# One-token attention over K and V of 537 MB: q spread by one matmul, half of K's sums in one PSUM bank, a third halving on VectorE, shared buffers

## Chip, cores and metric

One core of one Trainium2 chip runs the kernel; the other cores are idle. The metric is the device time of one execution in microseconds. The trace is one profiled execution; its span (1250.2 us before) is some 1.6 us shorter than the time of the same run.

## The reference

```python
B, H, Sq, Skv, Dh = 8, 32, 1, 4096, 128          # bf16
scores = einsum('bhqd,bhkd->bhqk', q, k) * Dh ** -0.5
out = einsum('bhqk,bhkd->bhqd', softmax(scores), v)
```

There are 256 independent heads with one query each. K and V are 268 MB each, and every byte is used once.

## The kernel before

A tile is 8 heads: 16 partitions per head, 256 positions in each partition, so K of a tile is [128, 256, 128] and 8.39 MB. There are 32 tiles and three slots for K and V together. VectorE multiplies K by q in place, halves the sum over d by additions, TensorE adds the rest with an identity matrix into PSUM (its output memory, used here in banks of 512 f32 values per partition), VectorE reduces each PSUM bank to scores, and ScalarE makes the weights. A loop on TensorE multiplies V by them. In the listing, `...` marks cuts.

```python
def q_prep(t):                       # q of 8 heads: pick, copy, spread, copy
    x, p0 = divmod(t * G, P)
    qh = ps_q.tile([G, D], F32, name="qh", tag="qp")
    nc.tensor.matmul(qh[:], lhsT=ident[:, p0 : p0 + G], rhs=q_all[:, x, :], start=True, stop=True)
    qg = q_pool.tile([G, D], BF16, name="qg", tag="qg")
    nc.scalar.activation(out=qg[:], in_=qh[:], func=ACT.Copy)
    qp = ps_q.tile([P, D], F32, name="qp", tag="qp")
    nc.tensor.matmul(qp[:], lhsT=heads..., rhs=qg[:], start=True, stop=True)
    ...
def width_of(t, u):                  # columns left for TensorE
    return D // 4 if u >= NU // 2 and 0 < t < NT - 3 else D // 2
def product(t, lo, hi):              # VectorE, in place in K
    ... part *= q
    ... part[:, :, 0:64] += part[:, :, 64:128]
    if width_of(t, lo // UC) < D // 2:
        ... part[:, :, 0:32] += part[:, :, 32:64]
def sum_over_d(t, u):                # 64 positions x 8 columns = one bank
    for s in range(width_of(t, u) // DS): nc.tensor.matmul(ps[:], lhsT=ident[:], rhs=...)
def scores_of(t, u):                 # 64 scores from one bank
    nc.vector.tensor_reduce(out=scs[t][:, u * UC : (u + 1) * UC], in_=..., axis=AX.X, op=ALU.add)
...
for t in range(NT):                  # tiles 1 to 29 ("loop")
    product(t, 0, 2 * Q); result_of(t - 2); q_prep(t + 2)
    sum_over_d(t, 0); sum_over_d(t, 1)
    product(t, 2 * Q, 3 * Q); sum_over_d(t, 2); scores_of(t, 0); scores_of(t, 1)
    product(t, 3 * Q, C); sum_over_d(t, 3); scores_of(t, 2)
    values_loop(t - 1); load("k", t + 1); load("v", t)
    scores_of(t, 3); weights_of(t); copy_of(t - 1)
```

## Time and profile before

| | before |
|---|---|
| time, median of 6 runs | 1251.88 us (1251.49 to 1252.03) |
| busiest engine | VectorE, 1021.9 us, 82% |
| loads | 536.94 MB, 99.5% of 16 engines' time |
| waiting of VectorE for K | 139.9 us in 28 tiles |

In the views, PE is TensorE, DVE VectorE, ACT ScalarE, POOL GpSimd, SPq the queue of SyncE from which the loads are issued, and L191 line 191 of the kernel; a name after `<-` in brackets is what ended the idle time. The prediction below shows the page's main lines. Views are added. First, the groups of instructions with shapes kept apart; the columns are instructions, busy us and mean ns, idle us before them. The prediction takes its 2292 ns from this line:

```profile
L194 DVE TENSOR_TENSOR kt<-kt 128x4096 bf16<-128x4096 bf16 x70 | 160.5, 2292 | 2.4
```

Second, two small queues of the page (packets, MB, share of 16 engines), called instruction, which move no data of the kernel.

```profile
q8 instruction: 15, 0.25, 0.1%
...
q14 instruction: 9, 0.07, 0.0%
```

Third, the timeline at the end of tile 15 (start, duration, idle before with its releaser). VectorE finishes its last addition at 616.46, reduces the third quarter, and then waits 1.35 us for the four matmuls of the fourth:

```profile
615.24 1.22 DVE L199 TENSOR_TENSOR kt<-kt 128x2048 bf16<-128x2048 bf16 x1
616.38 0.68 DVE L223 TENSOR_REDUCE sc<-ps 128x64 f32<-128x512 f32 x1
...
618.41 0.69 DVE L223 TENSOR_REDUCE sc<-ps 128x64 f32<-128x512 f32 x1 [1.35 <-PE ps L211]
```

### The profile page before, as it was taken

How to read it: one execution, taken by the hardware profiler on the slowest of the kernel's cores; microseconds unless marked ns; L12 is line 12 of the kernel's file. 1: busy time of each engine (PE TensorE's matmuls, PEld its weight loads, DVE VectorE, ACT ScalarE, POOL GpSimd, SP SyncE). 2: the span in 40 equal slices, each digit the busy share in tenths (PEclk: the TensorE clock that was granted, in tenths of full speed). 3: DMA queues.
4: the chain of work that ended last, by engine and by line, in shares of the span. 5: the costliest groups of instructions: out<-in, count | busy, mean ns of one | idle time of the engine just before them, and what ended most of it. 6: DMA issues, size and time to landing. Idle time of an engine off the chain costs nothing. (4 is left out here: it accounts for less than half of the span.)

```text
span 1250.2 us, 10842 instructions
## 1 busy us (share of the span) xinstructions
PE 786.8 (63%) x3116; PEld 299.6 (24%) x3116; DVE 1021.9 (82%) x495; ACT 166.1 (13%) x433; POOL 4.5 (0%) x24
## 2 busy tenths in 40 slices
PE   3366567666576655766558665577655776556755
PEld 1122123222232222322223222222222222212222
DVE  7887987878977789777798777987779877798783
ACT  0111011111011110111101111011110111101111
POOL 1000000000000000000000000000000000000000
PEclk9987788777888778877788777887778878779867
DMA  9999999999999999999999999999999999999997
GB/s 405 436 436 435 434 436 432 436 430 428 426 437 436 429 435 434 434 435 436 436 434 432 424 437 437 432 430 428 436 437 434 430 433 434 430 435 421 427 446 329
DMA packets 11432, 537.33 MB, mean 430 GB/s; under 512 B 1808, under 2 KB 2064, under 8 KB 2320
## 3 DMA queue, kind: packets, MB, share of 16 engines
q1 hardware_dynamic: 11072, 536.94, 99.5%
q8 instruction: 15, 0.25, 0.1%
q10 hardware_dynamic: 336, 0.07, 0.0%
q14 instruction: 9, 0.07, 0.0%
HBM read 536.94 MB, written 0.07 MB: 430 GB/s over the span
## 5 line engine op out<-in xcount | busy, mean ns | idle before, releaser
L191 DVE TENSOR_TENSOR kt<-kt,qb 128x8192 bf16<-128x8192 bf16 (+1 forms) x99 | 560.9, 5665 | 146.6 <-DMA kt<-in_k_dram 139.9
L211 PE MATMUL ps<-kt,ident 128*128 128x512 bf16 x800 | 278.4, 511 | 389.9 <-DVE kt L199 299.7
L294 PE MATMUL av<-vt,w 128*32 x1740 | 425.5, 397 | 4.6
L194 DVE TENSOR_TENSOR kt<-kt 128x4096 bf16<-128x4096 bf16 (+1 forms) x99 | 288.8, 2917 | 3.4
L294 PEld LDWEIGHTS av<-vt,w 128*32 x1740 | 173.4, 100 | 262.4 <-issue 119.5
L211 PEld LDWEIGHTS <-ident 128*128 128x128 bf16 x800 | 95.7, 120 | 565.4 <-issue 527.9
L223 DVE TENSOR_REDUCE sc<-ps 128x64 f32<-128x512 f32 x128 | 85.3, 685 | 54.0 <-PE ps L211 54.0
L248 ACT ACTIVATE e<-sc,nmax 128x256 bf16<-128x256 f32 x32 | 16.3, 508 | 706.7 <-DVE nmax L242 706.7
L255 ACT ACTIVATE w<-e,mine 128x256 bf16<-128x256 bf16 x256 | 105.6, 495 | 1.1
L199 DVE TENSOR_TENSOR kt<-kt 128x2048 bf16<-128x2048 bf16 x56 | 68.6, 1225 | 1.9
L351 ACT ACTIVATE comb<-av 32x512 bf16<-32x512 f32 (+1 forms) x32 | 18.8, 586 | 329.0 <-PEq L284 321.4
L280 PE MATMUL av<-vt,w 128*32 128x512 bf16 x116 | 47.2, 499 | 14.6 <-issue 13.1
L371 PE MATMUL op<-comb,pick 32*16 32x128 bf16 (+1 forms) x128 | 12.1, 213 | 20.7 <-ACT comb L351 20.7
L280 PEld LDWEIGHTS av<-vt,w 128*32 128x32 bf16 x116 | 6.9, 100 | 55.2 <-issue 55.2
L177 PE MATMUL qp<-qg,heads 8*128 8x128 bf16 x32 | 7.0, 217 | 16.7 <-ACT qg L175 16.7
L371 PEld LDWEIGHTS <-pick 32*16 32x16 bf16 (+1 forms) x128 | 8.7, 83 | 27.7 <-issue 27.3
L322 PE MATMUL av<-vt,w 128*32 128x512 bf16 x188 | 13.7, 418 | 2.3 <-DMA vt<-in_v_dram 2.3
L235 DVE TENSOR_REDUCE pmax<-sc 128x1 f32<-128x256 f32 x32 | 13.4, 420 | 1.1
L175 ACT ACTIVATE qg<-qh 8x128 bf16<-8x128 f32 x32 | 8.5, 266 | 33.5 <-PE qh L171 33.5
L171 PE MATMUL qh<-q_all,ident 128*8 128x128 bf16 x32 | 7.2, 225 | 8.7 <-DMA q_all<-in_q_dram 8.3
L179 ACT ACTIVATE qb<-qp 128x128 bf16<-128x128 f32 x32 | 8.9, 278 | 9.7 <-PE qp L177 9.7
L237 DVE TENSOR_SCALAR spread<-same,pmax 128x32 f32<-128x32 f32 x32 | 7.7, 242 | 1.1
(31 smaller groups left out, 47.7 us busy)
## 6 DMA issues: line engine op xcount, KB each, us to landing
kt<-in_k_dram SPq DMA_DIRECT2D x4, 4096.0 KB, 24.3
kt<-in_k_dram SPq DMA_DIRECT2D x4, 2048.0 KB, 13.0
vt<-in_v_dram SPq DMA_DIRECT2D x1, 4096.0 KB, 33.9
vt<-in_v_dram SPq DMA_DIRECT2D x1, 2048.0 KB, 38.5
vt<-in_v_dram SPq DMA_DIRECT2D x1, 1024.0 KB, 40.5
vt<-in_v_dram SPq DMA_DIRECT2D x1, 512.0 KB, 41.3
vt<-in_v_dram SPq DMA_DIRECT2D x31, 25.8
kt<-in_k_dram SPq DMA_DIRECT2D x29, 28.3
```

Of the source, the lines that this page charges most:

```text
L191: nc.vector.tensor_tensor(out=part, in0=part, in1=qb[:].to_broadcast([P, hi - lo, D]), op=ALU.mult)
L194: nc.vector.tensor_tensor(out=part[:, :, 0 : D // 2], in0=part[:, :, 0 : D // 2], in1=part[:, :, D // 2 : D], op=ALU.add,)
L199: nc.vector.tensor_tensor(out=part[:, :, 0 : D // 4], in0=part[:, :, 0 : D // 4], in1=part[:, :, D // 4 : D // 2], op=ALU.add,)
L211: nc.tensor.matmul(ps[:], lhsT=ident[:], rhs=kt[:, u * UC : (u + 1) * UC, s * DS : (s + 1) * DS], start=(s == 0), stop=(s == n - 1),)
L223: made = nc.vector.tensor_reduce(out=scs[t][:, u * UC : (u + 1) * UC], in_=sums.pop((t, u))[:], axis=AX.X, op=ALU.add)
L248: nc.scalar.activation(out=e[:], in_=sc[:], func=ACT.Exp, bias=nmax[:, 0:1], scale=scale, accum_out=esums[t // R][:, t % R : t % R + 1],)
L255: nc.scalar.activation(out=w[:, :, g, :], in_=e_g, func=ACT.Copy, scale=mine[:, 0, g : g + 1])
L280: pe.matmul(av, lhsT=wf[:, i * nw : (i + 1) * nw], rhs=vf[:, i * nv : (i + 1) * nv], **how)
L294: pe.matmul(av, lhsT=wf[:, bass.ds(ow + i * nw, nw)], rhs=vf[:, bass.ds(ov + i * nv, nv)], start=False, stop=False,)
L322: nc.tensor.matmul(avs[t][j * AG : (j + 1) * AG, :], lhsT=w[:, i, :, :], rhs=vt[:, c0 : c0 + CB, :], start=(i < TG), stop=(j not in group[ ...
L351: nc.scalar.activation(out=comb[0:n, :, :], in_=av[0:n, :, :], func=ACT.Copy)
L371: nc.tensor.matmul(ops[n][:], lhsT=pick[0:e, m, r, :], rhs=comb[0:e, m, :], start=(r == 0 and m == 0), stop=(r == R - 1 and m == CB - 1 an ...
```

## The change

Its intent: less TensorE and ScalarE work for q, fewer VectorE reductions, shorter TensorE sums at the end of a tile. The new q layout takes more space per partition, which the shared buffers pay for.

```diff
-    q_n = ... "(x p) d -> p x d", p=P
+    q_n = ... "(x p) d -> p x d", p=QP            # QP = 32
-    heads = consts.tile([G, G, PH], BF16, name="heads")
+    heads = consts.tile([QP, QP, PH], BF16, name="heads")
 def q_prep(t):
-    (matmul from ident, copy to qg, matmul from heads)
+    nc.tensor.matmul(qp[:], lhsT=heads[:, h0 : h0 + G, :]..., rhs=q_all[:, x, :], start=True, stop=True)
-    return D // 4 if u >= NU // 2 and 0 < t < NT - 3 else D // 2
+    return D // 8 if lo >= C // 2 and 0 < t < NT - 3 else D // 2
 def product(t, lo, hi):
+    n = D
+    while n > width_of(t, lo):
+        n //= 2
+        (add the upper n columns to the lower n)
 def sum_over_d(t, lo, hi):
+    ds = BANK // (hi - lo)                         # 128 positions x 4 columns in one bank
     ...
-    e: tag "e", comb: tag "comb", w_last: a constant, q_pool of 3
+    e and comb: tag "ec", w_last: tag "sc" of the scores, q_pool of 2
 for t in range(NT):                                # loop tiles
-    sum_over_d(t, 0); sum_over_d(t, 1) ... scores_of(t, 0); scores_of(t, 1)
+    sum_over_d(t, 0, HALF)             ... scores_of(t, 0, HALF)
-    q_prep(t + 2)
+    q_prep(t + 1)
```

More of the change, by code (lines that the diff above doesn't have):

```diff
@@ L43 @@
     scale = float(D) ** -0.5
-    UC = 64
-    DS = 512 // UC
-    NU = C // UC
+    BANK = 512
     CB = 4
@@ L49 @@
     NQ = NT // R
+    QP = 32
     TB = 32
@@ L53 @@
     assert (NV - 2 * EDGE) % LOOP == 0
-    assert LAST % CB == 0 and TG * AG == P and NH % P == 0 and P % G == 0 and TB % PH == 0 and C % CB == 0
-    q_n = q.rearrange("b h o d -> (b h o) d").rearrange("(x p) d -> p x d", p=P)
+    assert LAST % CB == 0 and TG * AG == P and NH % QP == 0 and QP % G == 0 and TB % PH == 0 and C % CB == 0
+    q_n = q.rearrange("b h o d -> (b h o) d").rearrange("(x p) d -> p x d", p=QP)
     o_n = out.rearrange("b h o d -> (b h o) d").rearrange("(n u x) d -> n x u d", u=OB, x=RG)
@@ L62 @@
     consts = ctx.enter_context(tc.tile_pool(name="consts", bufs=1))
-    q_pool = ctx.enter_context(tc.tile_pool(name="q_pool", bufs=3))
+    q_pool = ctx.enter_context(tc.tile_pool(name="q_pool", bufs=2))
     w_pool = ctx.enter_context(tc.tile_pool(name="w_pool", bufs=2))
@@ L72 @@
     ps_z = ctx.enter_context(tc.tile_pool(name="ps_z", bufs=1, space=bass.MemoryType.PSUM))
-    q_all = consts.tile([P, NH // P, D], BF16, name="q_all")
+    q_all = consts.tile([QP, NH // QP, D], BF16, name="q_all")
     ident = consts.tile([P, P], BF16, name="ident")
@@ L81 @@
     )
-    heads = consts.tile([G, G, PH], BF16, name="heads")
+    heads = consts.tile([QP, QP, PH], BF16, name="heads")
     nc.gpsimd.memset(heads[:], 0.0)
     nc.gpsimd.affine_select(
-        out=heads[:], in_=heads[:], pattern=[[-1, G], [0, PH]], compare_op=ALU.not_equal,
+        out=heads[:], in_=heads[:], pattern=[[-1, QP], [0, PH]], compare_op=ALU.not_equal,
         fill=1.0, base=0, channel_multiplier=1,
@@ L128 @@
     )
-    w_last = consts.tile([P, LAST, RG], BF16, name="w_last")
-    nc.gpsimd.memset(w_last[:], 0.0)
     loads = {}
@@ L168, in q_prep @@
     def q_prep(t):
-        x, p0 = divmod(t * G, P)
-        qh = ps_q.tile([G, D], F32, name="qh", tag="qp")
+        x, h0 = divmod(t * G, QP)
+        qp = ps_q.tile([P, D], F32, name="qp", tag="qp")
         nc.tensor.matmul(
-            qh[:], lhsT=ident[:, p0 : p0 + G], rhs=q_all[:, x, :], start=True, stop=True
-        )
-        qg = q_pool.tile([G, D], BF16, name="qg", tag="qg")
-        nc.scalar.activation(out=qg[:], in_=qh[:], func=ACT.Copy)
-        qp = ps_q.tile([P, D], F32, name="qp", tag="qp")
-        nc.tensor.matmul(qp[:], lhsT=heads[:].rearrange("g h x -> g (h x)"), rhs=qg[:], start=True, stop=True)
+            qp[:], lhsT=heads[:, h0 : h0 + G, :].rearrange("h g x -> h (g x)"), rhs=q_all[:, x, :],
+            start=True, stop=True,
+        )
         qb = q_pool.tile([P, 1, D], BF16, name="qb", tag="qb")
@@ L180, in q_prep, with width_of @@
         qbs[t] = qb
-    def width_of(t, u):
-        return D // 4 if u >= NU // 2 and 0 < t < NT - 3 else D // 2
+    def width_of(t, lo):
+        return D // 8 if lo >= C // 2 and 0 < t < NT - 3 else D // 2
     def product(t, lo, hi):
@@ L193, in product, with sum_over_d, scores_of @@
         )
-        nc.vector.tensor_tensor(
-            out=part[:, :, 0 : D // 2], in0=part[:, :, 0 : D // 2],
-            in1=part[:, :, D // 2 : D], op=ALU.add,
-        )
-        if width_of(t, lo // UC) < D // 2:
+        n = D
+        while n > width_of(t, lo):
+            n //= 2
             nc.vector.tensor_tensor(
-                out=part[:, :, 0 : D // 4], in0=part[:, :, 0 : D // 4],
-                in1=part[:, :, D // 4 : D // 2], op=ALU.add,
+                out=part[:, :, 0:n], in0=part[:, :, 0:n], in1=part[:, :, n : 2 * n], op=ALU.add
             )
     sums = {}
-    def sum_over_d(t, u):
+    def sum_over_d(t, lo, hi):
         kt = loads["k", t]
-        ps = ps_s.tile([P, UC, DS], F32, name="ps", tag="ps")
-        n = width_of(t, u) // DS
+        ps = ps_s.tile([P, BANK], F32, name="ps", tag="ps")
+        ds = BANK // (hi - lo)
+        n = width_of(t, lo) // ds
         for s in range(n):
             nc.tensor.matmul(
-                ps[:], lhsT=ident[:],
-                rhs=kt[:, u * UC : (u + 1) * UC, s * DS : (s + 1) * DS],
+                ps[:], lhsT=ident[:], rhs=kt[:, lo:hi, s * ds : (s + 1) * ds],
                 start=(s == 0), stop=(s == n - 1),
             )
-        sums[t, u] = ps
+        sums[t, lo] = ps
     scs = {}
-    def scores_of(t, u):
-        if u == 0:
+    def scores_of(t, lo, hi):
+        if lo == 0:
             scs[t] = sc_pool.tile([P, C], F32, name="sc", tag="sc")
+        ps = sums.pop((t, lo))[:].rearrange("p (c s) -> p c s", c=hi - lo)
         made = nc.vector.tensor_reduce(
-            out=scs[t][:, u * UC : (u + 1) * UC], in_=sums.pop((t, u))[:], axis=AX.X, op=ALU.add
+            out=scs[t][:, lo:hi], in_=ps, axis=AX.X, op=ALU.add
         )
-        if u == NU - 1:
+        if hi == C:
             behind_loop(made)
@@ L246, in weights_of @@
             esums[t // R] = small.tile([P, R], F32, name="esum", tag="esum")
-        e = o_pool.tile([P, C], BF16, name="e", tag="e")
+        e = o_pool.tile([P, C], BF16, name="e", tag="ec")
         nc.scalar.activation(
@@ L259, in weights_of @@
         if t == NT - 1:
+            w_last = sc_pool.tile([P, LAST, RG], BF16, name="w_last", tag="sc")
+            nc.gpsimd.memset(w_last[:], 0.0)
+            ws["last"] = w_last
             for i in range(LAST // CB):
@@ L347, in copy_of @@
     def copy_of(t):
-        comb = o_pool.tile([P, CB, D], BF16, name="comb", tag="comb")
+        comb = o_pool.tile([P, CB, D], BF16, name="comb", tag="ec")
         av = avs.pop(t)[:].rearrange("p (m d) -> p m d", d=D)
@@ L363, in last_rows @@
                 nc.tensor.matmul(
-                    ops[n][:], lhsT=w_last[:, i, :], rhs=loads["v", t][:, C - LAST + i, :],
+                    ops[n][:], lhsT=ws["last"][:, i, :], rhs=loads["v", t][:, C - LAST + i, :],
                     start=False, stop=(i == LAST - 1),
@@ L392, in store_of @@
             nc.scalar.dma_start(o_n[s, :, lo : u + 1, :], stages[s][:, lo : u + 1, :])
-    Q = C // 4
+    Q, HALF = C // 4, C // 2
     load("k", 0)
@@ L399 @@
         q_prep(0)
-        q_prep(1)
         for t in range(NT):
@@ L408 @@
                 load("v", t)
-            product(t, 0, 2 * Q if loop else Q)
-            if not loop:
-                sum_over_d(t, 0)
+            if loop:
+                product(t, 0, HALF)
+            else:
+                product(t, 0, Q)
+                sum_over_d(t, 0, Q)
             if 0 < t - 1 <= LT:
@@ L416 @@
                     result_of(t - 2)
-            if t + 2 < NT:
-                q_prep(t + 2)
+            if t + 1 < NT:
+                q_prep(t + 1)
             if loop:
-                sum_over_d(t, 0)
+                sum_over_d(t, 0, HALF)
             else:
-                product(t, Q, 2 * Q)
-            sum_over_d(t, 1)
-            if not loop:
-                scores_of(t, 0)
-            product(t, 2 * Q, 3 * Q)
-            sum_over_d(t, 2)
+                product(t, Q, HALF)
+                sum_over_d(t, Q, HALF)
+                scores_of(t, 0, Q)
+            product(t, HALF, HALF + Q)
+            sum_over_d(t, HALF, HALF + Q)
             if loop:
-                scores_of(t, 0)
-            scores_of(t, 1)
+                scores_of(t, 0, HALF)
+            else:
+                scores_of(t, Q, HALF)
             if t > 2 and t % R == 1:
                 recip_of(n)
-            product(t, 3 * Q, C)
-            sum_over_d(t, 3)
-            scores_of(t, 2)
+            product(t, HALF + Q, C)
+            sum_over_d(t, HALF + Q, C)
+            scores_of(t, HALF, HALF + Q)
             if loop:
@@ L441 @@
                 values_of(t - 1, 0, C)
-            scores_of(t, 3)
+            scores_of(t, HALF + Q, C)
             weights_of(t)
```

## The prediction

> **What bounds the kernel now.** I read the page from the top: busy shares, slices, DMA queues, then the groups of instructions, and after that the waits, the waits of the DMA queue, and the timeline of one tile.
>
> ```profile
> span 1250.2 us, 10842 instructions
> PE 786.8 (63%) x3116; PEld 299.6 (24%) x3116; DVE 1021.9 (82%) x495; ACT 166.1 (13%) x433; POOL 4.5 (0%) x24
> ...
> DMA  9999999999999999999999999999999999999997
> GB/s 405 436 436 435 434 436 432 436 430 428 426 437 436 429 435 434 434 435 436 436 434 432 424 437 437 432 430 428 436 437 434 430 433 434 430 435 421 427 446 329
> ...
> q1 hardware_dynamic: 11072, 536.94, 99.5%
> ```
>
> No compute engine is full: VectorE, the busiest, works 82% of the span. The row DMA has a 9 in every slice but the last, the loads' queue fills 99.5% of the time of 16 engines, and the rate is 421 to 437 GB/s from slice to slice. The loads are K and V, 2 x 256 x 4096 x 128 x 2 bytes = 536.9 MB, each byte read once. So the kernel looks bound by the volume of its loads.
>
> The packet records of the trace say it more sharply. Most of the volume comes in packets of 65536 bytes, whose median time is 2.42 us (5th to 95th percentile 2.418 to 2.427). Each of 16 engines moves 33.55 MB, which is 512 such packets: 512 x 2.42 = 1239 us. Counting packets in flight from record to record, all 16 engines have one from about 2 us after the start to about 1242 us. The rest of the 1250 us is the head (1 to 2 us until the first packets move), the tail (the engines run dry between 1242 and 1246 us, then the last rows of V, one copy and one store, some 5 us) and a few packets of up to 3.8 us. I put the dips of the GB/s row down to those packets and to where a slice cuts a long packet.
>
> VectorE does wait, and for what is telling:
>
> ```profile
> DVE kt L191 <- DMA kt<-in_k_dram: 139.9, 28, 6.3
> ...
> DVE sc L223 <- PE ps L211: 54.0, 33, 3.9
> ```
>
> In 28 tiles VectorE waits on average 5.0 us for the next K to land. It is ahead of the loads.
>
> What would make the change matter all the same is a load queue that runs empty because a buffer comes free late. There are three slots for K and V, so a load is issued when a slot is released. The timeline of a middle tile shows the two releases:
>
> ```profile
> 616.51 1.86 PE L211 MATMUL ps<-kt,ident 128*128 128x512 bf16 x4 [8.15 <-DVE kt L199]
> ...
> 618.41 0.33 SPq L158 DMA_DIRECT2D vt<-in_v_dram  x1
> ...
> 624.96 8.69 DVE L191 TENSOR_TENSOR kt<-kt,qb 128x16384 bf16<-128x16384 bf16 x1 [4.88 <-DMA kt<-in_k_dram]
> ...
> 635.26 0.33 SPq L158 DMA_DIRECT2D kt<-in_k_dram  x1
> ```
>
> V is issued at 618.41, the moment that the last TensorE sums have read K of this tile. The K ahead of it in the queue lands only at 624.96. Likewise K at 635.26 follows the loop over V. Setting the bytes issued against the bytes moved by then (issue times against packet records): 2.3 MB, or 5.3 us of work, are left when V is issued, and 3.4 MB, or 7.8 us, when K is. Over all steady tiles the smaller margin goes from 5.4 down to 3.6 us. It is never zero. Hence the queue does not run dry, and VectorE could be up to about 3 us per tile later before anything is lost.
>
> **What the Trainium skill says.** "DMA: Bandwidth & Descriptors", section "Where 436 GB/s comes from", derives a ceiling of 435.2 GB/s for the 16 ports into SBUF. The trace agrees: 2.42 us per 65536 bytes is 27.1 GB/s per engine, 433 GB/s for 16. "HBM Reference", section "Specifications (TRN2)", says that a core streaming alone goes well above its share of 358 GB/s, to about 425; here the mean is 430. "VectorE: DVE Perf Modes", section "Side-by-side: where the cycles go for N=2048 bf16", gives 1224 ns for 2048 elements at two per cycle; the trace has 1225 ns for the 128x2048 addition. For the new load of q, "DMA: Bandwidth & Descriptors", section "Why a DMA increments its semaphore by 16 and not by 1", says that the number of engines is the largest divisor up to 16 of the slowest dimensions: 32 partitions still give 16 engines; no run yet shows it.
>
> **The change part by part.** Durations are from these groups of the page:
>
> ```profile
> L191 DVE TENSOR_TENSOR kt<-kt,qb 128x8192 bf16<-128x8192 bf16 (+1 forms) x99 | 560.9, 5665 | 146.6 <-DMA kt<-in_k_dram 139.9
> L211 PE MATMUL ps<-kt,ident 128*128 128x512 bf16 x800 | 278.4, 511 | 389.9 <-DVE kt L199 299.7
> ...
> L223 DVE TENSOR_REDUCE sc<-ps 128x64 f32<-128x512 f32 x128 | 85.3, 685 | 54.0 <-PE ps L211 54.0
> ...
> L199 DVE TENSOR_TENSOR kt<-kt 128x2048 bf16<-128x2048 bf16 x56 | 68.6, 1225 | 1.9
> ...
> L175 ACT ACTIVATE qg<-qh 8x128 bf16<-8x128 f32 x32 | 8.5, 266 | 33.5 <-PE qh L171 33.5
> L171 PE MATMUL qh<-q_all,ident 128*8 128x128 bf16 x32 | 7.2, 225 | 8.7 <-DMA q_all<-in_q_dram 8.3
> ```
>
> 1. *Third halving on VectorE.* In tiles 1 to 28, both quarters of the second half get an addition of 64x16 = 1024 elements: 56 instructions. The 4096-element one takes 2292 ns and the 2048-element one 1225 ns; the difference is 0.521 ns per element, so 1024 elements should take 1225 - 1024 x 0.521 = 691 ns. That is +38.7 us of VectorE.
> 2. *First half in one bank.* In the 29 loop tiles two reductions of 512 inputs become one of 512 inputs to 128 outputs. I keep 685 ns, since the inputs are as many: 29 x 685 = -19.9 us of VectorE. The TensorE work stays: 16 matmuls of 512 columns either way.
> 3. *Fewer sums on TensorE.* 56 quarters go from 4 matmuls to 2: L211 falls from 800 to 688. The groups of four last 1.02 to 1.86 us in the timeline, about 0.36 us each: some -40 us of TensorE.
> 4. *q.* 32 matmuls (-7.2 us) and 32 copies on ScalarE (-8.5 us) go. At the start, the first multiplication waits for q's chain (until 9.53 us) and would begin about 0.6 us sooner; behind it the queue still holds both K tiles and a V, so no load comes sooner by it in a way that counts.
> 5. *Shared buffers.* The exponentials and the copy of the output sums share one buffer, q has two instead of three, and the zeroed weights for the last rows are made in the buffer of the last scores. The copy follows the eight weight scalings on the same engine, ScalarE, and the next exponential comes some 20 us after TensorE has read the copy; q is still prepared one tile ahead; the zeroing (302 ns) falls between the exponential (ending about 1234.2) and the last weights (about 1237.6). I expect no wait from any of them. Space is freed, but the slots for K and V stay three.
>
> Sum: VectorE 1021.9 + 38.7 - 19.9 = about 1041 us, TensorE about 740, ScalarE about 158. For the moment at which V is issued within a tile: + 2 x 0.69 (two halvings) - 0.685 (one reduction) - 0.85 (two matmuls less between the last addition and the release, at the 0.43 us spacing of the slow clock there) = -0.16 us, nearly nothing. The margin of about 5 us stays, no packet goes sooner or later, and the time stays: 1251.7 us.
>
> **The rivals.** *VectorE becomes the bound.* For it: it was the fullest engine and gets 19 us more. Against it: 0.65 us per tile against 5.0 us of waiting for K, and part of the wait for TensorE (54.0 us in total) shrinks too. If my estimate of the small addition were short by a factor of three, the margin would just be used up, and the time would rise by perhaps 5 to 30 us. *The kernel gets faster because TensorE or VectorE releases slots earlier.* For it: SP waits for them all the time. Against it: SP waits with work still queued, so an earlier issue only lengthens the queue; even a perfect stream needs 1239 us plus head and tail, so over 2% (below 1226.8 us) is shut off. *The sharing makes a new wait*, say the next exponential behind the copy of the sums: it would have to cost over 3 us per tile to show. *q on 32 partitions is slower to load:* 64 KB in 256 rows as before; doubling its packets' time would cost well under 1 us once.
>
> **Range and chances.** The runs of before spread by 0.4 us. Slow packets can differ by a microsecond or two from run to run, and the head and the tail could move by 1 us. That gives 1249.5 to 1254.0. Faster by over 2% would need fewer bytes or faster packets: 0.01. Slower by over 2% needs over 25 us from a wait I did not see: 0.02. The same: 0.97.
>
> **What would show it.** Right: DMA at 9 in all slices but the last, q1 near 99.5%, the wait of L183 (the multiplication's new line) for K still 130 to 155 us, the small additions at about 690 ns x56, 99 reductions, VectorE near 1041 us and the sums 688. Wrong: a reduction of 128x128 well over 685 ns, an addition near 1.2 us, a wait for K that vanishes while the DMA row shows gaps, or any long wait of ScalarE for the reader of the shared buffer.

## The result and the profile after

The changed kernel takes 1253.14 us (1252.68 to 1253.37, 6 runs) against 1251.88 us. The ratio is 1.001 with a 95% interval of 0.9997 to 1.0023: the same.

The page after, in the order of the first lines of the prediction (span, busy time of the engines, then by slice the DMA share in tenths and the rate, then the queues):

```profile
span 1251.0 us, 10646 instructions
...
PE 745.7 (60%) x2972; PEld 278.6 (22%) x2972; DVE 1043.5 (83%) x522; ACT 157.6 (13%) x401; POOL 5.3 (0%) x24
...
DMA  9999999999999999999999999999999999999997
GB/s 404 436 436 434 434 436 432 436 436 428 423 432 434 437 434 432 430 436 436 434 434 436 433 430 432 434 436 434 430 426 434 436 435 430 434 428 428 430 445 318
...
q1 hardware_dynamic: 11072, 536.94, 99.4%
...
q14 instruction: 10, 0.08, 0.0%
```

The row DMA has not moved by a digit. VectorE has 21.6 us more, TensorE 41.1 us less, ScalarE 8.5 us less, and the time does not follow any of them.

The groups after, shapes kept apart:

```profile
L201 PE MATMUL ps<-kt,ident 128*128 128x512 bf16 x688 | 240.4, 506 | 448.4 <-DVE kt L189 448.1
...
L189 DVE TENSOR_TENSOR kt<-kt 128x1024 bf16<-128x1024 bf16 x56 | 38.7, 692 | 1.9
L213 DVE TENSOR_REDUCE sc<-ps 128x128 f32<-128x512 f32 x29 | 19.8, 683 | 0.0
...
L166 PE MATMUL qp<-q_all,heads 32*128 32x128 bf16 x32 | 7.3, 229 | 8.6 <-DMA q_all<-in_q_dram 8.6
```

The new addition takes 692 ns, 56 times; the new reduction makes twice the scores in 683 ns.

The waits after (total us, times, longest):

```profile
DVE kt L183 <- DMA kt<-in_k_dram: 139.3, 28, 6.1
...
DVE sc L213 <- PE ps L201: 30.8, 33, 4.0
```

VectorE waits as long for K as before (139.9); its wait for TensorE has fallen from 54.0 to 30.8 us. The timeline of the same tile shows both sides of that exchange:

```profile
617.38 0.68 DVE L213 TENSOR_REDUCE sc<-ps 128x64 f32<-128x512 f32 x1
617.51 1.03 PE L201 MATMUL ps<-kt,ident 128*128 128x512 bf16 x2 [8.27 <-DVE kt L189]
618.58 0.33 SPq L153 DMA_DIRECT2D vt<-in_v_dram  x1
618.59 0.69 DVE L213 TENSOR_REDUCE sc<-ps 128x64 f32<-128x512 f32 x1 [0.53 <-PE ps L201]
...
624.99 8.69 DVE L183 TENSOR_TENSOR kt<-kt,qb 128x16384 bf16<-128x16384 bf16 x1 [4.73 <-DMA kt<-in_k_dram]
```

VectorE reaches the end of the tile 1.00 us later (617.38 against 616.38), TensorE then needs 1.03 us in place of 1.86, and V is issued at 618.58 against 618.41. The next K lands when it did.

### The profile page after: what moved, and what is told of

Its sections match the earlier page's. It is cut to its first block, busy times and chain, and to the rows that moved or that the text cites. A ratio compares the mean times of both kernels' runs of the same rounds, so it can differ in the third digit from the quotient of the medians.

```text
span 1251.0 us, 10646 instructions
## 1 busy us (share of the span) xinstructions
PE 745.7 (60%) x2972; PEld 278.6 (22%) x2972; DVE 1043.5 (83%) x522; ACT 157.6 (13%) x401; POOL 5.3 (0%) x24
## 5 line engine op out<-in xcount | busy, mean ns | idle before, releaser
L201 PE MATMUL ps<-kt,ident 128*128 128x512 bf16 x688 | 240.4, 506 | 448.4 <-DVE kt L189 448.1
L288 PE MATMUL av<-vt,w 128*32 x1740 | 429.8, 406 | 2.3
L189 DVE TENSOR_TENSOR kt<-kt 128x4096 bf16<-128x4096 bf16 (+3 forms) x211 | 396.2, 1878 | 7.2
L288 PEld LDWEIGHTS av<-vt,w 128*32 x1740 | 177.7, 102 | 260.1 <-issue 106.6
L201 PEld LDWEIGHTS <-ident 128*128 128x128 bf16 x688 | 72.1, 117 | 597.5 <-DVE kt L189 476.7
L213 DVE TENSOR_REDUCE sc<-ps 128x64 f32<-128x512 f32 (+1 forms) x99 | 67.9, 686 | 30.8 <-PE ps L201 30.8
L166 PE MATMUL qp<-q_all,heads 32*128 32x128 bf16 x32 | 7.3, 229 | 8.6 <-DMA q_all<-in_q_dram 8.6
L316 PEld LDWEIGHTS <-w 128*32 128x32 bf16 x188 | 6.2, 104 | 10.8 <-issue 7.8
L232 DVE TRANSPOSE_TENSOR_REDUCE nmax<-spread 128x1 f32<-128x32 f32 x32 | 6.8, 212 | 1.1
(27 smaller groups left out, 30.8 us busy)
```

Source lines behind the costliest of these rows:

```text
L189: nc.vector.tensor_tensor(out=part[:, :, 0:n], in0=part[:, :, 0:n], in1=part[:, :, n : 2 * n], op=ALU.add)
L201: nc.tensor.matmul(ps[:], lhsT=ident[:], rhs=kt[:, lo:hi, s * ds : (s + 1) * ds], start=(s == 0), stop=(s == n - 1),)
L213: made = nc.vector.tensor_reduce(out=scs[t][:, lo:hi], in_=ps, axis=AX.X, op=ALU.add)
L288: pe.matmul(av, lhsT=wf[:, bass.ds(ow + i * nw, nw)], rhs=vf[:, bass.ds(ov + i * nv, nv)], start=False, stop=False,)
L316: nc.tensor.matmul(avs[t][j * AG : (j + 1) * AG, :], lhsT=w[:, i, :, :], rhs=vt[:, c0 : c0 + CB, :], start=(i < TG), stop=(j not in group[ ...
```

## The experiments

Theory: the loads bind, and neither the VectorE work added nor the TensorE work removed lies on the path. Rival A: VectorE, the fullest engine, is as good as the bound. Rival B: the change saves real compute time that only this kernel's loads hide. Rival C: the 1.2 us between the medians, outside both spreads although inside the interval, come from a part of the change. Twelve kernels ran; medians of before beside them were 1251.55 to 1251.88 us.

### More VectorE work ahead of the release of K

In tiles 1 to 28, N extra instructions in the third quarter, on 64 positions x 64 columns of K. They take the maximum of each value with itself, so the result stays right, although the first halving still reads these columns (the expectation's "result unused" is not exact):

```diff
 def product(t, lo, hi):
     ...
+    if 0 < t < NT - 3 and lo == C // 2:
+        for _ in range(N):
+            nc.vector.tensor_tensor(out=part[:, :, D // 2 : D], in0=part[:, :, D // 2 : D],
+                in1=part[:, :, D // 2 : D], op=ALU.max)
```

N = 1: 

> The changed kernel with one extra VectorE instruction of 4096 elements (about 2.29 us, result unused) in tiles 1 to 28, ahead of the release of K: 28 x 2.29 = 64 us more VectorE work. Theory (the loads bound, VectorE has some 5 us per tile to spare, the smallest margin of the load queue is 3.4 us): time unchanged, 1252 to 1254.5 us, wait for K falls from 5.0 to about 2.7 us per tile. Rival (VectorE at 83% is as good as the bound): 1253 + 64 = 1317 us.

N = 2: 

> Two extra instructions, 4.6 us per tile. Theory: the wait for K falls to about 0.4 us per tile and the smallest queue margins (3.4 us) are overrun, so this is at the edge: 1253 to 1275 us. Rival (VectorE bound): 1253 + 128 = 1381 us. Rival (VectorE can never matter because the loads run by themselves): 1253 us.

N = 3: 

> Three extra instructions, 6.9 us per tile, more than the 5.0 us of waiting. Theory: VectorE is now the bound and adds (6.9 - 5.0) x 28 = 53 us: 1290 to 1325 us, no wait for K left. Rival (VectorE bound from the start): 1253 + 192 = 1445 us. Rival (never matters): 1253 us.

N = 4: 

> Four extra instructions, 9.2 us per tile. Theory: (9.2 - 5.0) x 28 = 117 us more, 1350 to 1390 us, that is 64 us over three of them: from the kink on every microsecond counts in full. Rival (VectorE bound from the start): 1253 + 256 = 1509 us. Rival (never matters): 1253 us.

| N | VectorE added per tile | time, median of 4 (N = 0: of 6) | over the changed kernel | ratio to before, 95% |
|---|---|---|---|---|
| 0 | 0 | 1253.14 us | 0 | 0.9997 to 1.0023 |
| 1 | 2.3 us | 1262.75 us | 9.6 us | 1.0067 to 1.0101 |
| 2 | 4.6 us | 1284.95 us | 31.8 us | 1.0240 to 1.0301 |
| 3 | 6.9 us | 1312.59 us | 59.5 us | 1.0476 to 1.0511 |
| 4 | 9.2 us | 1374.28 us | 121.1 us | 1.0962 to 1.0998 |

The full addition of rival A (64 us per step) is seen only from N = 3 to N = 4, where it is 61.7 us. Up to there most of the work is absorbed. N = 3 and N = 4 came out in the ranges of the theory. N = 1 and N = 2 did not: 8 and 10 us above the upper ends. The waits of N = 1, then of N = 3:

```profile
DVE kt L183 <- DMA kt<-in_k_dram: 73.6, 25, 4.5
```

```profile
DVE kt L183 <- DMA kt<-in_k_dram: 1.9, 5, 0.9
```

At N = 1 VectorE still waits 73.6 us for K, so it is not the bound, and yet the kernel is slower. The loads themselves have become slower. The packet records say how. I count packets of 65536 bytes that took over 2.7 us (the median is 2.42), their excess over 2.42 us divided by 16 engines, and the time for which engines have no packet, as a mean over the 16 (18.3 us in the changed kernel, nearly all of it before the program's first load and after the last):

| kernel | long packets | of them within 4 us after a V is issued | excess per engine | engines without a packet |
|---|---|---|---|---|
| before | 28 | 9 | 1.0 us | 17.0 us |
| changed | 24 | 5 | 0.8 us | 18.3 us |
| N = 1 | 225 | 181 | 9.4 us | 20.3 us |
| N = 2 | 397 | 330 | 16.1 us | 35.3 us |
| N = 3 | 428 | 412 | 18.4 us | 60.1 us |

The last column is counted from the first packet of the trace to its last. The two columns account for the growth of the traces' spans: at N = 1 they grow by 8.6 and 2.0 us, 10.6 against 10.9; at N = 2 by 15.3 and 17.0, 32.3 against 34.2; at N = 3 by 17.6 and 41.8, 59.4 against 58.9. At N = 1 the queue never ran empty as a whole: at the V of tiles 3 to 28 the backlog (bytes issued and not yet moved, packets in flight counted in part) was still 1.3 to 3.2 us, against 3.3 to 4.9 in the changed kernel. At N = 2 it went down to 0.1, and at N = 3 it was never above 0.2. My margin was wrong as a measure. A backlog that is an average over 16 engines is used up for some of them sooner.

The traces bear this out. At N = 3, after the V issued at 613.23, the first 16 packets start 0.95 to 1.57 us later and take 2.57 to 3.41 us, and the next 16 take 2.42 or 2.43: what is long is the first packet of each engine that had run dry. The trace shows 16 completions for each load, one by one. Of the 448 of K (16 in each of 28 tiles), 6 come less than 2.5 us after the issue of V in the kernel before (or ahead of it), 6 in the changed one, 169 at N = 1, 403 at N = 2 and all 448 at N = 3, beside 9, 5, 181, 330 and 412 long packets near a V. The limit of 2.5 us was chosen afterwards, and the packet records don't name their engine, so the two counts can't be matched engine by engine.

### The same work after the release of K

To separate late issue from VectorE's own traffic in memory, about as much work was put where VectorE waits anyway, on the scores after their last reader:

```diff
             weights_of(t)
+            if 0 < t < NT - 3:
+                for _ in range(5):
+                    nc.vector.tensor_tensor(out=sc[:], in0=sc[:], in1=sc[:], op=ALU.max)
```

> One extra instruction ahead of the release of K cost 9.7 us where none was expected, and most of the lengthened packets came within 4 us of the issue of a V. This run gives VectorE about as much extra work (5 instructions of 256 f32 elements, some 0.42 us each, 2.1 us per tile in 28 tiles), but after the release of K, in the time in which it waits for the next K anyway. Theory (a V issued later reaches the engines that are ahead too late; VectorE's work as such costs nothing): 1252.4 to 1254.5 us, some 40 lengthened packets as in the changed kernel, the wait for K down to about 2 us per tile. Rival (VectorE's traffic in memory slows the packets): about 1260 us and hundreds of lengthened packets.

It took 1252.91 us (1252.72 to 1253.03, 5 runs), ratio 1.0009. Its busy time and its wait for K:

```profile
PE 748.8 (60%) x2972; PEld 279.3 (22%) x2972; DVE 1103.1 (88%) x662; ACT 157.6 (13%) x401; POOL 5.3 (0%) x24
```

```profile
DVE kt L183 <- DMA kt<-in_k_dram: 56.3, 28, 3.3
```

VectorE has 59.6 us more than in the changed kernel, works 88% of the span as at N = 1 (1107.6 us), and waits 2.0 us per tile for K. The time has not moved, and 32 packets are long (12 near a V; 8 completions of K come less than 2.5 us after its issue). The "some 40 in the changed kernel" of the expectation is 24 by the count above. So the 10 us of N = 1 come from when V is issued. They do not come from how much VectorE does. Its traffic is not held equal here: these instructions are in f32, elsewhere, and move fewer bytes (15 KB per partition and tile against 24 KB, two inputs and the output counted). But at N = 1 the extra instruction starts 17.0 us before V is issued, and only 5 of the 225 long packets overlap it in time.

### Without the loads

The middle loads are left out and the first tiles' buffers used again. The result is wrong (relative error 1.07). A plainer cut, half of each load, reads what was never written.

```diff
     def load(kind, t):
+        if 1 < t < NT - 2 and kind == "k":
+            loads[kind, t] = loads[kind, t - 2]; return
+        if 0 < t < NT - 2 and kind == "v":
+            loads[kind, t] = loads[kind, 0]; return
```

In the kernel before: 

> The kernel before, but K of tiles 2 to 29 and V of tiles 1 to 29 are not loaded: the buffers of the first tiles are used again (wrong result on purpose). Theory (loads bound, compute needs about 33.7 us per tile against 38.7 of the loads): about 1085 us, 1060 to 1120. Rival (VectorE or TensorE bound): hardly below 1240 us.

In the changed kernel: 

> The same cut made in the changed kernel. Theory: the change is nearly neutral for the compute chain as well, -0.16 us per tile: 2 to 10 us below the kernel before with the same cut. Rival (the change saved real time that the loads hide): over 20 us below. Rival (the added VectorE work of 19 us counts in full): 15 to 25 us above.

In the changed kernel with `D // 4` for `D // 8`, so two halvings: 

> The same cut in the changed kernel with two halvings in place of three in the second half (the first half keeps its one bank). Theory: VectorE loses 38.7 us of additions and gets some 23 us of waiting for the longer TensorE sums back: about 16 us below the changed kernel with the cut, so the third halving costs more than it saves where loads don't bind. Rival (the third halving pays by relieving TensorE): above the changed kernel with the cut.

| | time, median of 4 |
|---|---|
| before, without the loads | 1114.30 us (1112.77 to 1114.68) |
| changed, without the loads | 1107.14 us (1106.30 to 1107.96) |
| changed, two halvings, without the loads | 1089.84 us (1088.98 to 1091.03) |

All are in the ranges set, though the first lies near the upper end of its own. The loads cost 138 us of the 1252: compute alone, with the last tiles' loads, needs 1114. Busy time and the wait of VectorE for the sums, in the order of the table:

```profile
PE 753.2 (68%) x3116; PEld 290.1 (26%) x3116; DVE 1019.5 (92%) x495; ACT 166.3 (15%) x433; POOL 4.5 (0%) x24
...
DVE sc L229 <- PE ps L217: 60.5, 44, 3.9
```

```profile
PE 699.0 (63%) x2972; PEld 268.3 (24%) x2972; DVE 1040.1 (94%) x522; ACT 157.8 (14%) x401; POOL 5.3 (0%) x24
...
DVE sc L219 <- PE ps L207: 31.4, 34, 4.0
```

```profile
PE 731.5 (67%) x3084; PEld 277.8 (26%) x3084; DVE 1001.4 (92%) x466; ACT 157.8 (15%) x401; POOL 5.3 (0%) x24
...
DVE sc L219 <- PE ps L207: 55.2, 34, 4.1
```

From the first to the second, VectorE works 20.6 us more and waits 29.1 us less: -8.5 us, and -7.2 was measured. From the second to the third it works 38.7 us less and waits 23.8 us more: -14.9 us, and -17.3 was measured. So the loads do hide a gain, but of 7 us. The third halving costs more than it saves. The rest of the change gains 24.5 us (1114.30 to 1089.84): the reductions' busy time falls by 18.3 us (86.3 to 68.0) and the wait for the sums by 5.3, which points to the one bank for the first half; the new q and the sharing were not tried alone without the loads.

### Parts of the change, with the loads

All with 5 rounds. The control is the changed kernel unaltered. One kernel has only the new q and the shared buffers (`D // 4`, two banks for the first half), one has only the sums (q and buffers as before), one undoes the third halving:

```diff
-        return D // 8 if lo >= C // 2 and 0 < t < NT - 3 else D // 2
+        return D // 4 if lo >= C // 2 and 0 < t < NT - 3 else D // 2
```

Control: 

> The changed kernel again, as a control for the difference of 1.2 us. Theory (a real difference of 0.1%, of the order of one slow engine in the tail): 1252.7 to 1253.4 us again, against 1251.5 to 1252.0 for before. Rival (chance of one session): within 0.4 us of before.

New q and sharing only: 

> Only the new q (one matmul from 32 partitions) and the shared buffers; sums and halvings as in the kernel before. If the 1.2 us come from q's load or from sharing: 1253 us. If they come from the sums: 1251.9 us. In both cases within 2 us of before, since the loads bind.

Sums only: 

> Only the sums: first half in one bank, three halvings in the second half; q and the buffers as in the kernel before. If the 1.2 us come from the sums: 1253 us. If they come from q or sharing: 1251.9 us. VectorE again near 1043 us busy, and no effect of it on the time.

Two halvings: 

> The changed kernel with two halvings in place of three: VectorE does 38.7 us less work, TensorE 112 matmuls more. Theory (loads bind): 1252 to 1253.5 us, the wait for K grows by some 0.6 us per tile to about 156 us in total. Rival (VectorE bound): about 1215 us.

| kernel | time, median of 5 | ratio to before, 95% |
|---|---|---|
| changed, again | 1252.84 us (1252.42 to 1253.00) | 0.9993 to 1.0020 |
| new q and sharing only | 1252.76 us (1252.60 to 1253.04) | 0.9994 to 1.0021 |
| sums only | 1252.49 us (1252.38 to 1252.63) | 0.9992 to 1.0019 |
| two halvings | 1251.59 us (1251.41 to 1251.75) | 0.9984 to 1.0011 |

By the intervals all four are the same as before (1251.82 us, 9 runs). The control fell in the theory's range. The two halvings came out 0.4 us below theirs. Taking 38.7 us off VectorE left the time where it was. The wait for K took up 17.1 us of it, the wait for the longer TensorE sums the rest (30.8 to 54.4 us):

```profile
DVE kt L183 <- DMA kt<-in_k_dram: 156.4, 29, 6.9
```

That ends rival A. As to rival C, neither half of the change carries the 1 us alone: each half has it, and the kernel with both but with two halvings has not. My either-or expectation failed. What does go with it is a count. The small queue q14 moves 8192 bytes now and then, and two series of such packets appear in every trace. Of one series, each packet (0.32 us) stands next to a load packet of 3.08 us in place of 2.42 (2.97 once, at 146 us of the kernel before). For the last ones, at 1152 and 1205 us, the neighbour is a packet of 32768 bytes, of 1.87 to 1.88 us in place of 1.21. That delays one DMA engine by some 0.98 us each time:

| trace | this series, us from the start | last packet of V lands |
|---|---|---|
| before | 146, 418, 707, 998 | 1246.20 us |
| two halvings | 146, 418, 707, 1000 | 1246.23 us |
| changed | 127, 379, 651, 901, 1152 | 1247.14 us |
| changed, again | 126, 379, 651, 901, 1152 | 1247.03 us |
| sums only | 127, 379, 651, 901, 1152 | 1247.05 us |
| new q and sharing only | 146, 418, 668, 940, 1205 | 1247.19 us |
| work after the release | 105, 321, 552, 785, 979 | 1246.98 us |

Four such packets go with 1246.2 us, five with 1247.0 to 1247.2. The completions of one load by the 16 engines lie 0.3 us apart in the first transfers. In the changed kernel the last falls behind the first by 3.3 us before the packet at 901 and by 4.2 after it, by 3.6 before that at 1152 and by 4.6 after it; in the kernel before, which has none at 1152, the distance stays at 3.6. The last engine sets the end. The Trainium skill ("DMA: Bandwidth & Descriptors", section "Queues, rings and completion order") calls queue row 14 runtime-internal. The page of the trace calls it instruction. That the fifth packet is the cause fits all seven traces but was not tried by itself (the other small queue, q8, has 14 packets with the two halvings as in the slower ones), and which engine's program asks for these packets stays open.

No version beats the kernel before. The one with two halvings equals it here.

## Why the prediction was right

**What bounds.** Right. The volume of the loads fixes the time: the row DMA stays at 9, and 38.7 us less VectorE work gives nothing.

**The parts.** The addition was put at 691 ns and took 692; the reduction at 685 and took 683. The sums went to 688 matmuls and lost 38.0 us against 40 predicted; TensorE as a whole came to 745.7 us and not 740, with 4.3 us more in the loop over V (425.5 to 429.8). ScalarE came out at 157.6 us. VectorE was put at 1041 us and came to 1043.5: 85.3 us of reductions became 67.9, a saving of 17.4 and not of 19.9, since the records of neighbouring reductions overlap and two in a row were already counted short. q's chain began the first multiplication at 9.20 us against 9.53, 0.3 us sooner and not 0.6, because q landed 0.3 us later. No wait for the shared buffers appeared.

**The moment at which V is issued.** The sum said -0.16 us; in the tile shown V comes 0.17 us later by the clock, and 0.14 us later relative to the landing of K. The two matmuls saved 0.83 us against 0.85 worked out. The extra addition costs 0.73 us from start to start, not 0.69, and the dropped reduction gives back 0.60, not 0.685: +0.03 us. The rest is there at the start already, since VectorE began its second multiplication of this tile 0.14 us later. Over tiles 3 to 28 the backlog at V's issue lies between 3.3 and 4.9 us, against 3.4 and 4.9 before. (The prediction's 5.3 and 7.8 us at the two issues shown, and its 5.4 down to 3.6, come out as 4.6, 7.1 and 4.9 down to 3.4 when packets in flight are counted in part.)

**A side step that failed.** The text says "VectorE could be up to about 3 us per tile later before anything is lost". It is false: 2.3 us per tile cost 9.6 us. The step took the backlog of 16 engines as one number. The completions of one load spread over 2 to 3 us in the middle of the run, so the engines that are ahead have less left than the mean, and a packet lasts 2.42 us. What the runs show is that long packets multiply after late issues of V, in step with the engines that have finished K by then, and that about as much work elsewhere costs nothing. Where between 0.2 us and 2.3 us per tile the loss begins was not measured. The time was right because the change moved V by 0.1 to 0.2 us only; there was less room than I believed, and a change that moved V by 2 us would have been predicted wrongly by this step.

**The rivals.** VectorE as the bound fell with the two halvings and with the work after the release. An earlier release as a gain fell too: with the two halvings V of the tile shown is issued at 618.00 in place of 618.41, and the time is that of before. The rival of a faster kernel had 7 us in it, visible without the loads. The sharing and the load of q made no wait that shows.

## What to carry to other kernels

Where the loads' queue is full from end to end, judge a change of compute only by what it does to the moment at which buffers come free. Measure the room by adding work ahead of that release, not by the waits of the busiest engine: here VectorE waited 5 us per tile, but an added 2.3 us was already not wholly free. Cut the loads out to see what a change is worth in itself, and try each of its parts there, since one part may pay for another's loss.

## What the Trainium skill lacked or had wrong

- "DMA: Bandwidth & Descriptors", section "Where 436 GB/s comes from", says that for loads from HBM the HBM side, about 358 GB/s, binds, although it also notes a 16 MB transfer at 425. On this core alone the loads ran at 430 GB/s over 1250 us and 27.1 GB/s per engine: close to the port ceiling that the same section derives, and not held at 358.
- No page says that a load queue can be too short without being empty. With a mean backlog of 1.3 us or more at every issue, 225 packets in place of 24 took over 2.7 us, and the kernel lost 9.6 us. The first packet of an engine that had run dry took about 3.1 us in place of 2.42.
- No page gives how far the 16 DMA engines drift apart in a long stream. Completions of one load lay 0.3 us apart at the start and 3.6 us (before) to 4.6 us (changed) apart at the end.
- "DMA: Bandwidth & Descriptors", section "Queues, rings and completion order", names row 14 as runtime-internal, and no page gives what its packets cost a full stream. Here an 8192-byte packet of 0.32 us went with a neighbour of 3.08 us in place of 2.42, and five of them in place of four went with an end 0.8 to 1.0 us later.
